# Taking sums of squares of later weights along with the projections, and giving VectorE two attention units a head

## The chip, the cores and the metric

The kernel runs on one core of one Trainium2 chip, in one launch. The metric is the device time of one execution in microseconds (us). Comparisons are made between runs on the same chip.

## The reference

Two layers, each an attention block and a gated block, over x of 2048 rows by 448 columns, all in float32. The weights are the same in both layers.

```python
def A(x, wqkv, wo):            # 16 heads of 28
    q, k, v = split(x @ wqkv)
    p = softmax(q @ k.T * 28 ** -0.5)
    return (p @ v) @ wo
def B(x, w_gate, w_up, w_down): # 448 -> 1792 -> 448
    return (sigmoid(x @ w_gate) * (x @ w_up)) @ w_down
for layer in range(2):
    x = x + A(layernorm(x), wqkv, wo)
    x = x + B(layernorm(x), w_gate, w_up, w_down)
```

## The kernel before

The 2048 rows are 4 blocks of 512, each 4 tiles of 128. Every product is made from float16 parts: an operand is scaled by a power of two and cut into a high and a low part, and three products of parts are added up in PSUM. The order of the instructions on each engine is the order in which the program calls them; there is no scheduler. An engine runs its queue in order and waits by semaphores.

A layer runs through four stages: `project` (queries, keys and values), `attend`, `out_project` and `gated`.

**project.** `qk(b, blk, fill, before)` makes the queries and keys of block b as 7 products of 128 columns (11 matmuls each). After each product ScalarE writes the high part and its squares, VectorE the low part (L723) and the larger of two halves of the squares (L727), SyncE stores both parts in DRAM (`qk_scr`), and then the entry of `fill` for that product is called, which is other work put in at that place. Products go in turn through 4 PSUM banks, so a product waits until the one four before it has been read. Three products later TensorE adds up the squares (`norm_products`, L701 and L704); the last three of a block are added up in `finish`, which is called as `fin` inside a later step. `vals(b, blk, after)` makes the values of the block's four tiles, and calls entries of `after` in the same manner. In layer 0 blocks 0 and 1 are turned by TensorE; blocks 2 and 3 are normed, transposed in 32x32 pieces on VectorE (`squares`), stored in DRAM (`store`, L317), gathered back as columns (`gather`, L325 and L327) and cut into parts by ScalarE and VectorE (`ready`, L210 to L216). The order is qk(0), vals(0), qk(1), vals(1), qk(2), qk(3), vals(2), vals(3). The guard for the exponent is computed from the norms during vals(2), and attention starts behind vals(3).

**attend.** For 16 heads and 16 key tiles of 128 there are 4 units, one for each block of queries: 1024 units of 128x512. TensorE makes the scores of three units at a time (`score`, L1129), and ScalarE takes their exponential in one instruction (L1144). FEW tells for layer 0 how many units of each head go to VectorE instead, 1, 2 or 3 (3 in layer 1 throughout); ASIDE gives for each number the key tile at which the unit is begun, and the key tile and query block that it is: `score_aside`, ten VectorE instructions (L1154 to L1163). `mix` multiplies the probabilities of a key tile with its values (L1180), some two groups behind the scores. An aside unit uses the PSUM bank in which the sums of the previous head stood and those of the next will stand. `finish(h)` turns and divides the head's sums on VectorE (L1209 to L1215). When `mix` is through with key tile c, counted through all heads to 256, it calls `along(c)`.

**Prepare.** In layer 0 `along(c)` also runs the preparation of the later weights. `Prepare.__init__` writes a list of steps with the key tile at which each is due. First come 12 steps that measure: wo, four pieces of w_down and seven pieces of w_gate beside w_up, each read on GpSimd's DMA queue, with a sum of squares on VectorE (L1018, two for a gate-and-up piece) and a copy of it (L1020). They lie 4 or 5 key tiles apart. Then `sizes` adds up over the partitions on GpSimd (L1032) and VectorE makes the powers of two. Then 22 steps that split: wo, 7 pairs of w_down rows, and 14 of w_gate and w_up columns, 5, 8 and 7 key tiles apart. Each is read on GpSimd's queue, summed, scaled and cut on VectorE (L1012, L1070, L221, L226) and stored (`gu_parts`, `dn_parts`, `o_parts`).

`big` hands out 19 buffers of 8 KB a partition, the one longest free first; a DMA into a buffer waits on its queue until the readers before it are done.

## Time and profile before

| what | us |
|---|---|
| median of three runs | 1918.15 |
| range of the three | 1917.75 to 1919.35 |
| the profiled execution | 1918.24 |
| its span, first to last instruction | 1916.4 |
| TensorE busy | 1897.9 |
| VectorE busy | 1412.8 |
| ScalarE busy | 1366.0 |
| GpSimd busy | 240.6 |

A row of the timeline gives the start, the time, the engine, the line, the operation, out<-in, the count, and in brackets the idle time ahead of it and what ended it. A row of groups gives the line, engine, operation, tiles, shape and count, then the busy time and the mean ns of one, then the idle time ahead. A row of windows gives for a stretch the busy time and count for each engine, then the granted clock of TensorE, the busy share of the DMA engines and GB/s. In rows of one line's durations these are ns, least, median and most. Engines: PE TensorE, PEld its weight loads, DVE VectorE, ACT ScalarE, POOL GpSimd, SP SyncE. TensorE's granted clock was 0.997.

### The profile page before, as it was taken

How to read it: one execution, taken by the hardware profiler on the slowest of the kernel's cores; microseconds unless marked ns; L12 is line 12 of the kernel's file. 1: busy time of each engine (PE TensorE's matmuls, PEld its weight loads, DVE VectorE, ACT ScalarE, POOL GpSimd, SP SyncE). 2: the span in 40 equal slices, each digit the busy share in tenths (PEclk: the TensorE clock that was granted, in tenths of full speed). 3: DMA queues.
4: the chain of work that ended last, by engine and by line, in shares of the span. 5: the costliest groups of instructions: out<-in, count | busy, mean ns of one | idle time of the engine just before them, and what ended most of it. 6: DMA issues, size and time to landing. Idle time of an engine off the chain costs nothing. (4 is left out here: it accounts for less than half of the span.)

```text
span 1916.4 us, 56353 instructions
## 1 busy us (share of the span) xinstructions
PE 1897.9 (99%) x24317; PEld 1405.8 (73%) x24317; DVE 1412.8 (74%) x2816; ACT 1366.0 (71%) x1742; POOL 240.6 (13%) x467
## 2 busy tenths in 40 slices
PE   9999999999999999999999999999999999999999
PEld 4455655555566798999954568778888777899998
DVE  7648798687877598788663487778778667887764
ACT  5569999999983455454344799999999645555541
POOL 2013312232001111212100000000000011211110
PEclk9999999999999999999999999999999999999999
DMA  5575555345313657656634312122111235665752
GB/s 173 165 207 162 155 157 149 117 144 149 92 62 92 235 189 263 219 221 236 232 94 132 89 51 51 28 51 51 41 37 66 75 98 215 216 270 198 270 204 90
DMA packets 107298, 275.20 MB, mean 144 GB/s; under 512 B 12766, under 2 KB 63086, under 8 KB 106912
## 3 DMA queue, kind: packets, MB, share of 16 engines
q0 software_dynamic: 33088, 165.74, 24.5%
q1 hardware_dynamic: 73616, 105.54, 19.3%
q8 instruction: 192, 3.15, 0.7%
q14 instruction: 66, 0.54, 0.1%
q10 hardware_dynamic: 336, 0.23, 0.0%
HBM read 213.39 MB, written 50.73 MB: 138 GB/s over the span
## 5 line engine op out<-in xcount | busy, mean ns | idle before, releaser
L1144 ACT ACTIVATE prob_s<-sc 128x1536 f32<-128x1536 f32 x659 | 892.7, 1484 | 6.7 <-PE sc L1129 3.3
L1180 PE MATMUL acc<-prob_s,val_s 128*32 128x256 f32 (+3 forms) x7754 | 590.1, 383 | 0.0
L1129 PE MATMUL sc<-qp_s 114*32 114x512 f16 x7896 | 575.8, 379 | 0.0
L545 PEld LDWEIGHTS <-gu_s 128*128 128x128 f16 x4368 | 428.0, 98 | 60.3 <-issue 8.1
L1129 PEld LDWEIGHTS <-qp_s 114*32 114x32 f16 x8192 | 309.9, 96 | 176.3 <-issue 78.2
L1180 PEld LDWEIGHTS acc<-prob_s,val_s 128*32 128x32 f32 x7754 | 317.9, 110 | 100.8 <-issue 7.6
L545 PE MATMUL chain<-xwide_s,gu_s 128*128 128x256 f16 x2016 | 249.0, 273 | 4.1 <-DMA gu_s<-gu_parts 4.0
L1454 PE MATMUL dnp<-dn_s,hparts_s 128*128 128x224 f16 x2100 | 235.5, 259 | 0.0
L1454 PEld LDWEIGHTS <-hparts_s 128*128 128x128 f16 x2100 | 202.1, 98 | 4.8
L1527 ACT COPY one_q<-chain 128x256 f32<-128x256 f32 x224 | 82.0, 372 | 132.0 <-PE chain L545 131.3
L1160 DVE SCALAR_TENSOR_TENSOR power_q<-power_q,expo_q 128x512 f32<-128x512 f32 x222 | 153.7, 692 | 7.6
L545 PE MATMUL side<-xshort_s,gu_s 128*128 128x256 f16 x1120 | 142.1, 274 | 3.0 <-DVE one_q L1543 2.7
L530 PE MATMUL qkp<-xhl_s,wqk_s 128*128 128x512 f16 x616 | 138.0, 379 | 0.7 <-DVE xhl_s L509 0.3
L1543 DVE TENSOR_TENSOR one_q<-side,one_q 128x512 f32<-128x512 f32 x112 | 72.0, 684 | 83.4 <-PE side L545 83.4
L530 PEld LDWEIGHTS <-wqk_s 128*128 128x128 f16 x616 | 60.0, 98 | 70.1 <-ACT wqk_s L223 1.0
L1209 DVE STREAM_TRANSPOSE oturned_q<-acc 128x512 f32<-128x512 f32 x32 | 22.9, 717 | 118.4 <-PE acc L1180 118.4
L1345 POOL DMA_DIRECT2D gu_s<-gu_parts x104 | 56.0, 540 | 365.7 <-PE side L545 183.3
L545 PE MATMUL side<-xwide_s,gu_s 128*128 128x256 f16 x672 | 92.3, 274 | 0.0
L1407 ACT CAST hparts_s<-hsums_q 128x256 f16<-128x256 f32 (+1 forms) x144 | 68.4, 489 | 33.1 <-DVE hsums_q L1419 20.6
L722 ACT ACTIVATE qkhl_q<-qkp 128x512 f16<-128x512 f32 x56 | 33.2, 593 | 75.0 <-PE qkp L530 71.6
L1180 PE MATMUL acc<-power_q,val_s 128*32 128x256 f32 (+3 forms) x278 | 86.4, 393 | 0.0
L1554 ACT ACTIVATE one_q<-one_q 128x512 f32<-128x512 f32 x56 | 35.3, 630 | 71.3 <-DVE one_q L1543 71.2
(209 smaller groups left out, 2291.0 us busy)
## 6 DMA issues: line engine op xcount, KB each, us to landing
gu_s<-gu_parts POOLq DMA_DIRECT2D x104, 800.0 KB, 6.0
dn_s<-dn_parts POOLq DMA_DIRECT2D x50, 784.0 KB, 7.2
qp_s<-qk_scr SPq DMA_DIRECT2D x96, 224.0 KB
qk_scr<-qkhl_q SPq DMA_DIRECT2D x56, 256.0 KB
gu_parts<-pack_s POOLq DMA_DIRECT2D x14, 800.0 KB, 4.2
xt_scr<-xs_s SPq DMA_DIRECT2D x48, 224.0 KB
xraw_s<-xt_scr SPq DMA_DIRECT2D x12, 768.0 KB
qp_s<-qk_scr SPq DMA_DIRECT2D x64, 112.0 KB
```

The costliest lines, as they stand in the source:

```text
L530: nc.tensor.matmul(pm, w, x, start=(i == 0), stop=(i == len(terms) - 1))
L545: nc.tensor.matmul(pm, a, x, start=(first and i == 0), stop=(i == len(terms) - 1), skip_group_check=True)
L1129: nc.tensor.matmul(ps[32 * j:32 * j + 32, :], hd.k[:, keys], hd.q[:, qb * W:(qb + 1) * W], start=True, stop=True, tile_position=(0, 32 * j))
L1144: nc.scalar.activation(prob[:, 0:n, :], ps[:, 0:n, :], AF.Exp, scale=exp_scale)
L1160: nc.vector.scalar_tensor_tensor(p, p, c[k], y, op0=ALU.add, op1=ALU.mult)
L1180: nc.tensor.matmul(acc[qb * VC:(qb + 1) * VC, s], v[:, kc % TB, h, :], probs[c * NB + qb][:, s], start=(kc == 0 and a == 0), stop=(kc == N ...
L1345: queue.dma_start(self.gu[-1][m], gu_parts[p, m])
L1407: nc.scalar.copy(to[:, :, 0], a)
L1454: nc.tensor.matmul(pm, a[:, x, t], w[:, p, y], start=(begin and n == 0 and (j == 0 or alone)), stop=(n == 2), skip_group_check=True)
L1527: nc.scalar.copy(to, pm)
L1543: nc.vector.tensor_tensor(one[m], side[m], one[m], op=ALU.add)
L1554: nc.scalar.activation(out, v, AF.Sigmoid, scale=gate_scale)
```

## The change

The 12 measuring steps leave attention and go into the projections of layer 0, as a class `Measure`. Its reads are put at the value products of block 0 (six: wo, the four of w_down, the first gate-and-up piece) and at qk(2) (the other six). Its sums are put at the value products of block 1 (wo and the first of w_down), at qk(2) (five) and at qk(3) (five). Of a gate-and-up piece, the gate's squares are summed on VectorE and the up's on ScalarE, and one reduction on VectorE adds up the latter. `ready` of block 3 moves from the second and third product of qk(2) to the third and fourth. `fin` of block 1 stays where it was.

In attention, `sizes` is due at key tile 6 and the first split at 7; splits of w_down are 11 key tiles apart and those of gate and up 10, so that the last is due at 219 and the end at 229. FEW becomes two units for every head but the last, which keeps three: 33 in all, where it was 26.

```diff
@@ -63,7 +63,7 @@
 
 
 ASIDE = {1: ((6, 15, 1),), 2: ((4, 10, 3), (9, 15, 1)), 3: ((4, 9, 3), (8, 13, 1), (12, 15, 2))}
-FEW = "2221212111111233"
+FEW = "2222222222222223"
 
 
 TAIL = (0, 1, 3, 2, 5, 4, 6)
@@ -731,7 +731,8 @@
                 qrt.put(hl)
                 late.append(lambda i=i, sq=sq: norm_products(i, sq))
                 if i < len(fill) and fill[i]:
-                    fill[i]()
+                    for do in fill[i] if isinstance(fill[i], tuple) else (fill[i],):
+                        do()
 
             def finish():
                 while late:
@@ -799,10 +800,12 @@
                 b1.turned_low()
 
             fill = [idle, idle, lambda: b1.norm([0, 1]), lambda: b1.norm([2, 3]), idle, scaled]
-            along_values = {0: lambda: (b1.parts(), turned([0, 1])),
-                            1: lambda: (turned([2, 3]), big.put(b1.xn)),
-                            2: lambda: (fin(), b2.norm()),
-                            3: lambda: (b2.squares(), b2.store())}
+            tell = Measure()
+            add = tell.add
+            along_values = {0: lambda: (b1.parts(), turned([0, 1]), tell.read(2)),
+                            1: lambda: (turned([2, 3]), big.put(b1.xn), tell.read(2)),
+                            2: lambda: (fin(), b2.norm(), tell.read()),
+                            3: lambda: (b2.squares(), b2.store(), tell.read())}
         else:
             ones_of_values()
             fill = [idle, lambda: b1.ready(0, 1), lambda: b1.ready(2, 3), b2.norm,
@@ -817,9 +820,17 @@
         else:
             fill = [idle, lambda: b2.ready(0, 1), lambda: b2.ready(2, 3), b3.store]
         fin = qk(1, b1, fill, None)
-        vals(1, b1, {0: b3.gather, 2 if layer == 0 else 1: fin})
-        fin = qk(2, b2, [idle, lambda: b3.ready(0, 1), lambda: b3.ready(2, 3)], None)
-        fin = qk(3, blks[3], [], fin)
+        if layer == 0:
+            more = lambda: add(1)
+            vals(1, b1, {0: b3.gather, 1: add, 2: fin, 3: add})
+            fin = qk(2, b2, [more, more, lambda: (b3.ready(0, 1), tell.read()),
+                             lambda: b3.ready(2, 3), more, more, more], None)
+            fin = qk(3, blks[3], [add] * 5, fin)
+            assert not tell.rows
+        else:
+            vals(1, b1, {0: b3.gather, 1: fin})
+            fin = qk(2, b2, [idle, lambda: b3.ready(0, 1), lambda: b3.ready(2, 3)], None)
+            fin = qk(3, blks[3], [], fin)
         if layer > 0:
             big.put(*wq.qk)
         else:
@@ -883,6 +894,55 @@
                 big.put(wq.v)
 
         return values, heads, last_values
+
+    class Measure:
+
+
+
+        def __init__(self):
+            nc.vector.memset(sums[:, 3:7], 0.0)
+            self.part = cpool.tile([P, 2], F32, name="part", tag="part", bufs=1)
+            self.ups = cpool.tile([P, 7], F32, name="ups", tag="ups", bufs=1)
+            self.junk = big.get("junk", [P, 2048], BF16)
+            self.to_read = deque([("o", 0)] + [("d", j) for j in range(4)] + [
+                ("gu", j) for j in range(7)])
+            self.rows = deque()
+
+        def read(self, n=1):
+            for _ in range(n):
+                kind, j = self.to_read.popleft()
+                t = big.get("raw", [P, 2048])
+                n = {"o": 4, "d": min(4, NF - 4 * j), "gu": 0}[kind]
+                v = t[:, 0:n * D].rearrange("p (s n) -> p s n", n=D)
+                if kind == "gu":
+                    v = t.rearrange("p (w s c) -> p w s c", w=2, s=4)
+                    for i, w in enumerate((w_gate, w_up)):
+                        load_rows(v[:, i], w, j * 2 * P, 2 * P, nc.gpsimd)
+                elif kind == "o":
+                    load_rows(v, wo, 0, D, nc.gpsimd)
+                else:
+                    nc.gpsimd.dma_start(v, w_down[j * 512:j * 512 + n * P, :].rearrange(
+                        "(s p) n -> p s n", p=P))
+                self.rows.append((kind, j, t, n * D))
+
+        def add(self, read=0):
+            kind, j, t, n = self.rows.popleft()
+            m, n = {"o": (3, n), "d": (6, n), "gu": (4, 1024)}[kind]
+            v = t[:, 0:n]
+            nc.vector.tensor_tensor_reduce(self.junk[:, 0:n], v, v, 1.0, sums[:, m:m + 1],
+                                           op0=ALU.mult, op1=ALU.add,
+                                           accum_out=self.part[:, 0:1])
+            nc.vector.tensor_copy(sums[:, m:m + 1], self.part[:, 0:1])
+            if kind == "gu":
+                junk = qrt.get("junk", [P, 1024], BF16)
+                nc.scalar.activation(junk, t[:, 1024:2048], AF.Square,
+                                     accum_out=self.ups[:, j:j + 1])
+                qrt.put(junk)
+            big.put(t)
+            self.read(read)
+            if not self.rows and not self.to_read:
+                nc.vector.tensor_reduce(sums[:, 5:6], self.ups, axis=AX.X, op=ALU.add)
+                big.put(self.junk)
 
     def true_maxima(h):
 
@@ -913,25 +973,16 @@
 
 
         def __init__(self):
-            nc.vector.memset(sums[:, 3:7], 0.0)
-            self.part = cpool.tile([P, 2], F32, name="part", tag="part", bufs=1)
             self.raws, self.packs = big.ring(2), big.ring(2)
             self.halves, self.half = None, 0
-            tiles = [("o", 0)] + [("d", j) for j in range(4)] + [("gu", j) for j in range(7)]
-            order = [(self.measure, what) for what in tiles] + [
-                (self.split, what) for what in tiles[:1] + [("w", p) for p in range(NP)] + [
-                    (w, p) for p in range(NP) for w in ("g", "u")]]
-            self.read(*tiles[0])
-            self.steps = deque()
-            at = 6
-            for i, (do, what) in enumerate(order):
-                then = order[i + 1][1] if i + 1 < len(order) else None
-                self.steps.append((at, lambda do=do, what=what, then=then:
-                                   self.step(do, what, then)))
-                at += ((5 if what[0] == "gu" else 4) if do == self.measure else
-                       {"o": 5, "w": 8}.get(what[0], 7))
-                if i == len(tiles) - 1:
-                    self.steps.append((at, self.sizes))
+            order = [("o", 0)] + [("w", p) for p in range(NP)] + [
+                (w, p) for p in range(NP) for w in ("g", "u")]
+            self.read(*order[0])
+            self.steps = deque([(6, self.sizes)])
+            at = 7
+            for what, then in zip(order, order[1:] + [None]):
+                self.steps.append((at, lambda what=what, then=then: self.step(what, then)))
+                at += {"o": 5, "w": 11}.get(what[0], 10)
             self.steps.append((at, self.end))
             self.pack = None
 
@@ -954,14 +1005,11 @@
                 self.next = big.at(self.raws, "raw", [P, 2048])
             if kind == "o":
                 load_rows(self.view(self.next, kind), wo, 0, D, nc.gpsimd)
-            elif kind == "gu":
-                for i, w in enumerate((w_gate, w_up)):
-                    load_rows(self.view(self.next, kind)[:, i], w, j * 2 * P, 2 * P, nc.gpsimd)
             elif kind == "w":
                 for z in range(2):
                     r = slice((z * NP + j) * P, (z * NP + j + 1) * P)
                     nc.gpsimd.dma_start(self.view(self.next, kind)[:, z], w_down[r])
-            elif kind in "gu":
+            else:
                 v, w = self.view(self.next, kind), {"g": w_gate, "u": w_up}[kind]
                 for z in range(2):
                     c = slice((z * NP + j) * P, (z * NP + j + 1) * P)
@@ -969,30 +1017,20 @@
                                         w[0:384, c].rearrange("(s p) n -> p s n", p=P))
                     nc.gpsimd.dma_start(v[0:64, 3, z], w[384:448, c])
                 nc.gpsimd.memset(v[64:P, 3], 0.0)
-            else:
-                n = self.count(j)
-                nc.gpsimd.dma_start(self.view(self.next, kind)[:, 0:n, :],
-                                    w_down[j * 512:j * 512 + n * P, :].rearrange(
-                                        "(s p) n -> p s n", p=P))
-
-        def count(self, j):
-            return min(4, NF - 4 * j)
 
         def view(self, t, kind):
-            if kind == "gu":
-                return t.rearrange("p (w s c) -> p w s c", w=2, s=4)
             if kind in "gu":
                 return t[:, 0:1024].rearrange("p (s z n) -> p s z n", s=4, z=2)
             if kind == "w":
                 return t[:, 0:2 * D].rearrange("p (z n) -> p z n", z=2)
             return t[:, 0:4 * D].rearrange("p (s n) -> p s n", s=4)
 
-        def step(self, do, what, then):
+        def step(self, what, then):
             raw = self.next
             self.write()
             if then:
                 self.read(*then)
-            do(raw, *what)
+            self.split(raw, *what)
             if what == ("w", 0):
                 big.free.append(self.raws.popleft())
 
@@ -1011,22 +1049,6 @@
                                  (s34[:, 1], l12, s12[:, 1], ALU.subtract)):
                 nc.vector.tensor_tensor(to, a, b, op=op)
             return s12, s34
-
-        def add(self, m, v):
-            junk = big.at(self.packs, "junk", [P, 2048], BF16)
-            n = v.free_size()
-            nc.vector.tensor_tensor_reduce(junk[:, 0:n], v, v, 1.0, sums[:, m:m + 1],
-                                           op0=ALU.mult, op1=ALU.add, accum_out=self.part[:, 0:1])
-            nc.vector.tensor_copy(sums[:, m:m + 1], self.part[:, 0:1])
-
-        def measure(self, raw, kind, j):
-            if kind == "o":
-                self.add(3, raw[:, 0:4 * D])
-            elif kind == "gu":
-                self.add(4, raw[:, 0:1024])
-                self.add(5, raw[:, 1024:2048])
-            else:
-                self.add(6, raw[:, 0:self.count(j) * D])
 
         def sizes(self):
             nc.gpsimd.partition_all_reduce(size[:, 3:7], sums[:, 3:7], channels=P,
```

## The prediction, made before the changed kernel ran

> **What bounds the kernel now.** I read the share of busy time first, then the windows of the two attention stages, then the timeline at their edges, and last the waits and DMA shares of the first projection stage, since the change takes work from one of these stages and gives it to another. Base: the profiled execution took 1918.24 us, its span is 1916.4, and the median of the three runs is 1918.15, so the sum against the execution holds for the median within 0.1.
>
> ```profile
> core 0: us, PE busy (x) PEld busy (x) DVE busy (x) ACT busy (x) POOL busy (x), PEclk, DMA share, GB/s
> 119.10:570.70 451.60, 451.56 (x8140) 259.63 (x8139) 363.46 (x703) 448.63 (x333) 95.73 (x156) 1.00 0.48 141
> 1068.50:1515.10 446.60, 446.60 (x8108) 357.37 (x8107) 344.54 (x572) 444.04 (x326) 0.00 (x0) 1.00 0.18 46
> L1144 ACT ACTIVATE prob_s<-sc 128x1536 f32<-128x1536 f32 x333 | 448.6, 1514 | 3.7 <-DMA qp_s<-qk_scr 3.1 <-PE sc L1129 0.3
> ```
>
> The first two rows are the attention stages of layer 0 and layer 1, from first score product to first output projection. In layer 0 ScalarE runs 333 exponentials back to back, 448.63/333 = 1.347 us each, and sat idle only 3.7 us, of which 3.1 before the first. So ScalarE bounds that stage. Layer 1 does the same products with 48 units beside it on VectorE instead of 26, so with 326 exponentials, and takes 446.6: nearly the floor that TensorE's products set. VectorE is at 363.46/451.6 = 80% in layer 0.
>
> ```profile
> 105.17 0.49 PE L704 MATMUL knorm<-sq_q,ind 128*128 128x256 bf16 x3
> 119.10 1.48 PE L1129 MATMUL sc<-qp_s 114*32 114x512 f16 x24
> 67.40:104.40 37.00, 37.00 (x181) 17.51 (x179) 16.08 (x35) 19.46 (x33) 0.00 (x0) 1.00 0.47 140
> ```
>
> The projection ahead of it is TensorE's: in its second half (last row) TensorE is busy 37.0 of 37.0 us, VectorE only 16.08. The squared-norm products of the last block start at 105.17, in the middle of the value products, and the first scores follow the value products directly at 119.10. Whatever makes TensorE wait before 119.10 is added to the whole.
>
> **The change: fewer exponentials.** FEW goes from a sum of 26 to a sum of 33, so 7 more units of 128x512 leave ScalarE. 1024 - 26 = 998 units are 332.7 groups of three, 1024 - 33 = 991 are 330.3. The gain is 2.33 x 1.347 = 3.1 us, and the stage would take 448.5. That is above the 446.6 of layer 1, so TensorE doesn't yet cap it. The 0.6 us of other idle time of ScalarE is the most that could come on top: 3.7.
>
> **What VectorE has to do for it.**
>
> ```profile
> 214.89 0.75 DVE L1154 TENSOR_SCALAR expo_q<-aside,base 128x512 f32<-128x512 f32 x1 [2.86 <-PE aside L1129]
> 221.18 1.28 DVE L1018 CUSTOM_DVE_ANT_0 junk_s<-raw_s,sums 128x1024 bf16<-128x1024 f32 x1
> 222.72 1.29 DVE L1018 CUSTOM_DVE_ANT_0 junk_s<-raw_s,sums 128x1024 bf16<-128x1024 f32 x1
> 142.75 2.08 DVE L1018 CUSTOM_DVE_ANT_0 junk_s<-raw_s,sums 128x1792 bf16<-128x1792 f32 x1
> 145.05 2.08 DVE L1018 CUSTOM_DVE_ANT_0 junk_s<-raw_s,sums 128x1792 bf16<-128x1792 f32 x1
> L1018 DVE CUSTOM_DVE_ANT_0 junk_s<-raw_s,sums x19: 1145/1285/2085, 142.7 to 225.8; 128x1024 bf16<-128x1024 f32 x14, 128x1792 bf16<-128x1792 f32 x4, 128x896 bf16<-128x896 f32 x1
> 376.70 0.72 DVE L1209 STREAM_TRANSPOSE oturned_q<-acc 128x512 f32<-128x512 f32 x1 [6.86 <-PE acc L1180]
> 380.29 0.42 DVE L1012 TENSOR_TENSOR sums_q<-raws_s 128x256 f32<-128x256 f32 x1
> 386.06 0.75 DVE L1154 TENSOR_SCALAR expo_q<-aside,base 128x512 f32<-128x512 f32 x1
> 233.45 0.17 DVE L238 TENSOR_SCALAR pw<-size 128x4 int32<-128x4 int32 x1 [6.15 <-POOL size L1032]
> ```
>
> From start to start, a unit takes 6.29 us (214.89 to 221.18), a sum with its copy 1.54 (1024 wide), 2.30 (1792 wide) or 1.4 (896 wide, 1.145 and the same 0.25), the end of a head 3.6 and one gate or up split 5.8. Seven units add 44.0 us; 14 x 1.54 + 4 x 2.30 + 1.4 = 32.2 leave, so VectorE rises by 12 to 375 of 448.5, 84%. The sums are now done long before the powers of two are asked for at key tile 6, so the 6.15 us in which VectorE waited for GpSimd's all-reduce should go too; that was no one's critical wait.
>
> Spreading is what makes room: a gate or up split falls every 10 key tiles, not every 7. A key tile lasts 448.5/256 = 1.75 us, a head 28.0; a head with two splits holds 2 x 6.3 + 3.6 + 2 x 5.8 = 27.8, and averages over neighbours are 25.6. A unit is asked for six key tiles before its use and the products trail the scores by 2.25 groups, 10.5 + 3.0 = 13.5 us; a unit behind a split that has just begun is ready after 5.8 + 6.3 = 12.1. Thin, but it holds; I cost it at nothing. If this cover fails, TensorE waits. The last split ends at key tile 229 instead of 220, and the output weights are first read in the last head, from tile 242: nothing.
>
> **What the projection gets.** Twelve reads go onto GpSimd's queue from the first values on. GpSimd idles 14.30 and 9.05 us ahead of its two norm steps there (first rows below), a read of six issues lasts 3.63 (rows further below), and each read takes a buffer already free, or freed as named below, so the norm steps behind them aren't held up. ScalarE gets seven squares of 1024.
>
> ```profile
> 44.17 0.20 POOL L283 TENSOR_SCALAR rs<-mv 128x4 f32<-128x4 f32 x1 [14.30 <-DVE mv L280]
> 54.53 0.19 POOL L283 TENSOR_SCALAR rs<-mv 128x4 f32<-128x4 f32 x1 [9.05 <-DVE mv L280]
> L599 ACT ACTIVATE junk_s<-wraw_s 128x1792 bf16<-128x1792 f32 x2 | 3.4, 1682 | 0.0
> 66.71 0.41 DVE L740 TENSOR_REDUCE peaks<-qnorm 16x1 f32<-16x256 f32 x1
> 77.79 1.14 ACT L210 CAST xhl_s<-xraw_s 128x512 f16<-128x512 f32 x2 [3.15 <-DMA xraw_s<-xt_scr]
> 78.44 1.29 DVE L211 TENSOR_TENSOR xhl_s<-xraw_s,xhl_s 128x512 f16<-128x512 f32 x2 [3.47 <-ACT xhl_s L210]
> 82.06 0.69 DVE L723 SCALAR_TENSOR_TENSOR qkhl_q<-qkp,qkhl_q 128x512 f16<-128x512 f32 x1
> 82.87 0.69 DVE L723 SCALAR_TENSOR_TENSOR qkhl_q<-qkp,qkhl_q 128x512 f16<-128x512 f32 x1
> ```
>
> A square of 1024 lies under the 1.68 us of 1792, about 1.0, and ScalarE has 37.0 - 19.5 = 17.5 us free in the second half: nothing. VectorE gets 2.30 x 4 + 1.4 + 7 x 1.54 = 21.4 us into 37.0 - 16.1 = 20.9 of idle time. So it becomes full, and order decides. Ahead of block 3's parts stand, from 66.7: four sums (9.2), the peaks (0.8) and three evacuation pairs of 0.81 (82.06 to 82.87), 12.4 in all, to 79.1. The gathered block 3 used to land at 77.79 and now is asked for one product later. From its landing: one cast (0.6), four low parts (2.6), 11 evacuation pairs (8.9), a 896 and seven 1024 sums (12.2), peaks (0.8), 25.1 us. The last squares must be there when the norm products start, at 105.2. So the gather may land as late as 80.1 at no cost, and from there each microsecond is one that TensorE waits.
>
> ```profile
> 66.00:69.00 3.00, 3.00 (x18) 1.66 (x17) 1.42 (x3) 1.42 (x4) 0.00 (x0) 1.00 0.93 213
> 69.00:72.00 3.00, 3.00 (x16) 1.36 (x14) 0.36 (x1) 1.14 (x3) 0.00 (x0) 1.00 0.82 186
> 75.00:78.00 3.00, 3.00 (x16) 1.35 (x15) 0.00 (x0) 0.21 (x1) 0.00 (x0) 1.00 1.03 331
> 65.56 3.43 SPq L317 DMA_DIRECT2D xt_scr<-xs_s  x4
> 72.30 0.38 SPq L325 DMA_DIRECT2D xraw_s<-xt_scr  x1
> 173.05 0.78 POOL L203 DMA_DIRECT2D raw_s<-in_B_w_gate_dram  x1 [3.88 <-DVE sums L1020]
> 176.68 0.78 POOL L203 DMA_DIRECT2D raw_s<-in_B_w_gate_dram  x1
> raw_s<-in_B_w_down_dram POOLq DMA_DIRECT2D x1, 896.0 KB, 13.5
> ```
>
> Block 3's store (from 65.56) fills the DMA engines to 0.93 and 0.82, its gather (issued 72.30 when the store has landed) to 1.03. The second gate-and-up read takes block 2's gathered buffer, free at 66.7, so its six issues (3.63 us, 173.05 to 176.68) go out beside that store; the third takes the buffer that the store reads, and goes out beside the gather. Each is 2 x 384 KB, 0.79 MB: 2.4 us of all engines at 331 GB/s, 4.2 at 186. Before, nothing on GpSimd's queue ran there. Bounds: 0 if the reads fit the gaps, 8.4 us if both go wholly ahead at the slow rate. That sharing delays is shown by the last row: 896 KB took 13.5 us to land in the crowded stretch at 119. I take shares alike: 2.4 on the store, and half of it, 1.3, on the gather, whose rival is issued only bit by bit: it lands at 81.5 and costs 1.4 us.
>
> The Trainium skill (DMA: Bandwidth & Descriptors, Queues, rings and completion order) says that each DMA engine goes round between the queues it has work for, a packet at a time. By that rule this read is not behind the gather but between its packets, which speaks against the change; no row here shows the two queues at once in this stretch.
>
> Sum: 1918.2 - 3.1 + 1.4 = 1916.5.
>
> **The rivals.** (1) No collision: the reads fit the gaps, the gather lands by 80.1, and ScalarE's 0.6 us of idle time may go too: 1914.5 to 1915.1. For it: 20 us windows before show DMA shares of a half on average (0.47 in the row above). Against: the shares at that very place. (2) Slower: the reads go ahead. The place is block 3's store and gather, the price 1 us for each microsecond past 80.1, and it decides from 80.1 + 3.1 = 83.2; at 8.4 us late it lands at 86.2, costs 6.1 and gives 1921.2. More reads follow at once, so it could be still later. For it: the 13.5 us landing. Against: the gather's own queue is served meanwhile. The round-robin rule of the Trainium skill, named above, with larger packets in the reads than in the store, leans to this one. (3) VectorE's queue in attention: heads with two splits have 0.2 us to spare, so operations 10% longer would put each some 2.5 us behind; at two to three such heads 5 to 8 us, less the gain: 1921 to 1925. Against: layer 1's 344.54 busy us with three units a head stall nothing. (4) That the change doesn't do what it says: TensorE, not ScalarE, paces layer 0. Then 451.6 would stay: 1919.6. The 333 exponentials with 0.6 us between them speak against it.
>
> **How the numbers follow.** About 0.2% (3.8 us, so 1914.4 and 1922.1) is what a measurement of this kernel can tell from no change. Chances: forecast 0.46 (own range 1915.1 to 1918.2), (1) 0.20, (2) 0.23, (3) 0.08, (4) 0.03. Faster by over 0.2% is the lower half of (1), with the spread of the runs: 0.12. Slower is half of (2), most of (3) and what I can't see, 0.22. The range, 1914.4 to 1923, leaves out a tenth at each end.
>
> **What would show it.** Right: 331 exponentials in a stage of some 448.5 us; no wait of TensorE on an `aside` unit; the L210 wait for xraw in the third product longer than before, landing near 81.5; TensorE waiting about 1.4 us on sq at the last norm products; first scores at about 120.5. Wrong: first scores at 119.1 (then 1) or past 122 (then 2); a stage still over 450 us (then 3 or 4), told apart by ScalarE's idle time.

## The result, and the profile after

The changed kernel takes 1922.63 us (median of 8 runs, 1920.91 to 1926.01), the kernel before 1915.94 beside it (median of 8, the three of the forecast among them). The ratio of the runs is 1.0038, 95% interval 1.0026 to 1.0049: slower by some 7 us. The forecast was 1916.5; 1922.63 lies inside its range, which reached up to 1923 for the rivals' sake, and the sign was wrong. The profiled execution took 1920.91, its span is 1917.8.

The attention of layer 0 gained more than forecast. From first scores to first output projection it takes 446.86 us where it took 451.61, with 331 exponentials, and TensorE is busy throughout (windows and the group of the exponential, changed kernel):

```profile
core 0: us, PE busy (x) PEld busy (x) DVE busy (x) ACT busy (x) POOL busy (x), PEclk, DMA share, GB/s
125.66:572.52 446.86, 446.86 (x8109) 265.79 (x8108) 374.38 (x715) 444.23 (x331) 64.38 (x107) 1.00 0.40 117
L1166 ACT ACTIVATE prob_s<-sc 128x1536 f32<-128x1536 f32 (+1 forms) x331 | 444.2, 1515 | 3.4 <-PE sc L1151 3.1 <-DMA qp_s<-qk_scr 0.3
```

But the first scores come at 125.66, not 119.10: 6.56 us are lost ahead of attention. The timeline of SyncE's queue and of ScalarE shows block 3's store, gather and first cast:

```profile
66.76 3.46 SPq L317 DMA_DIRECT2D xt_scr<-xs_s  x4
77.97 0.38 SPq L325 DMA_DIRECT2D xraw_s<-xt_scr  x1
83.17 1.14 ACT L210 CAST xhl_s<-xraw_s 128x512 f16<-128x512 f32 x2 [4.59 <-DMA xraw_s<-xt_scr]
```

The gather is issued at 77.97 (72.30 before) and the cast starts at 83.17 (77.79). From the store's issue to the gather's it takes 11.2 us instead of 6.7: the reads did delay the store, by 4.5 us where 2.4 were forecast. What follows from it for TensorE is small, one wait for VectorE at the norm products of block 2 (timeline of TensorE):

```profile
92.65 0.27 PE L704 MATMUL knorm<-sq_q,ind 128*128 128x256 bf16 x1 [0.35 <-DVE sq_q L727]
```

The long wait comes 17 us behind that one (timeline of ScalarE, then of TensorE, then windows; `...` marks rows left out):

```profile
101.95 1.06 ACT L938 ACTIVATE junk_q<-raw_s 128x1024 bf16<-128x1024 f32 x1 [0.63 <-DMA raw_s<-in_B_w_up_dram]
...
106.84 1.06 ACT L938 ACTIVATE junk_q<-raw_s 128x1024 bf16<-128x1024 f32 x1 [2.59 <-DMA raw_s<-in_B_w_up_dram]
...
107.90 0.58 ACT L722 ACTIVATE qkhl_q<-qkp 128x512 f16<-128x512 f32 x1
108.51 0.63 ACT L725 ACTIVATE sq_q<-qkhl_q 128x512 bf16<-128x512 f16 x1
109.04 0.58 ACT L722 ACTIVATE qkhl_q<-qkp 128x512 f16<-128x512 f32 x1
109.66 0.63 ACT L725 ACTIVATE sq_q<-qkhl_q 128x512 bf16<-128x512 f16 x1
```

```profile
109.51 0.27 PE L704 MATMUL knorm<-sq_q,ind 128*128 128x256 bf16 x1 [1.99 <-DVE sq_q L727]
110.66 0.37 PE L704 MATMUL knorm<-sq_q,ind 128*128 128x256 bf16 x1 [0.88 <-DVE sq_q L727]
```

```profile
102.00:105.00 3.00, 3.00 (x16) 1.42 (x15) 2.64 (x7) 2.22 (x4) 0.16 (x1) 1.00 0.97 331
105.00:108.00 3.00, 2.52 (x15) 1.32 (x14) 1.15 (x3) 1.16 (x3) 0.00 (x0) 1.00 0.39 132
108.00:111.00 3.00, 0.61 (x3) 0.35 (x3) 2.42 (x8) 2.22 (x4) 0.00 (x0) 0.82 0.19 66
111.00:114.00 3.00, 3.00 (x12) 1.22 (x10) 0.81 (x4) 0.54 (x1) 2.03 (x2) 0.61 0.80 228
109.90:113.31 3.41, 2.65 (x8) 1.13 (x8) 1.88 (x8) 0.93 (x2) 1.34 (x2) 0.50 0.72 207
```

ScalarE waits 2.59 us, until 106.84, for the last up piece, and behind that square stand the last two evacuations of queries and keys. Their squares are what TensorE's last norm products wait for: TensorE is busy 0.61 of 3 us. Then its granted clock is 0.82 and 0.61 in the means of two 3-us windows; the last row, cut to the fall itself, has 0.50 for 3.41 us. That is 1.7 us of lost work if TensorE has work throughout; here it had 2.65 us of it, so 1.3 to 1.7. The 6.56 us add up as follows: 1.2 are there already at block 3's store (66.76 against 65.56), 0.9 come between the store and the first of the last norm products (107.25 against 105.17), and 4.5 behind that, which are the 2.9 us of gap and the clock.

The loss ahead of attention and the gain in it make 6.56 - 4.75 = 1.8 us, and the spans differ by 1.4, but the medians by 6.7. The two executions don't stand for their medians: that of before took 2.3 us more than its median of 1915.94, that of after is the shortest of its 8. And one stage that wasn't touched has grown: from the first output projection to layer 1's first scores (570.71 to 1068.47 before, 572.52 to 1072.81 after) 500.29 us instead of 497.76.

### The profile page after: what moved, and what is told of

Same layout as the page of the kernel before. It is cut to its first block, busy times and chain, and to the rows that moved or that the text cites. A ratio compares the mean times of both kernels' runs of the same rounds, so it can differ in the third digit from the quotient of the medians.

```text
span 1917.8 us, 56351 instructions
## 1 busy us (share of the span) xinstructions
PE 1893.8 (99%) x24285; PEld 1348.4 (70%) x24285; DVE 1442.2 (75%) x2866; ACT 1368.1 (71%) x1754; POOL 239.0 (12%) x467
## 5 line engine op out<-in xcount | busy, mean ns | idle before, releaser
L1166 ACT ACTIVATE prob_s<-sc 128x1536 f32<-128x1536 f32 (+1 forms) x657 | 887.7, 1485 | 7.3 <-PE sc L1151 3.4
L1202 PE MATMUL acc<-prob_s,val_s 128*32 128x256 f32 (+3 forms) x7700 | 574.2, 384 | 0.0
L1151 PE MATMUL sc<-qp_s 114*32 114x512 f16 x7868 | 557.0, 379 | 0.0
L1151 PEld LDWEIGHTS <-qp_s 114*32 114x32 f16 x8192 | 281.5, 96 | 195.2 <-issue 81.9
L1202 PEld LDWEIGHTS acc<-prob_s,val_s 128*32 128x32 f32 x7700 | 282.8, 110 | 133.4 <-issue 11.1
L1182 DVE SCALAR_TENSOR_TENSOR power_q<-power_q,expo_q 128x512 f32<-128x512 f32 x243 | 168.2, 692 | 8.3
L1202 PE MATMUL acc<-power_q,val_s 128*32 128x256 f32 (+3 forms) x300 | 94.2, 396 | 0.0
L1176 DVE TENSOR_SCALAR expo_q<-aside,base 128x512 f32<-128x512 f32 x81 | 60.6, 749 | 28.2 <-PE aside L1151 27.7
```

The costliest lines, as they stand in the source:

```text
L1151: nc.tensor.matmul(ps[32 * j:32 * j + 32, :], hd.k[:, keys], hd.q[:, qb * W:(qb + 1) * W], start=True, stop=True, tile_position=(0, 32 * j))
L1166: nc.scalar.activation(prob[:, 0:n, :], ps[:, 0:n, :], AF.Exp, scale=exp_scale)
L1176: nc.vector.tensor_scalar(y, ps, base2[:, 0:1], -126.0, op0=ALU.mult, op1=ALU.max)
L1182: nc.vector.scalar_tensor_tensor(p, p, c[k], y, op0=ALU.add, op1=ALU.mult)
L1202: nc.tensor.matmul(acc[qb * VC:(qb + 1) * VC, s], v[:, kc % TB, h, :], probs[c * NB + qb][:, s], start=(kc == 0 and a == 0), stop=(kc == N ...
```

## The experiments

Ratios are to the kernel before on the same chip, with 95% intervals, from 5 to 12 runs of each kernel and 15 to 33 of the kernel before. Stage times are those of one traced execution of each kernel.

### Both kernels once more

> The changed kernel once more, unchanged, for a second trace and times on the same chip as the other experiments. If the loss is where the first trace has it: first scores 124.5 to 126.5 us, ScalarE waiting for the last up piece, attention of layer 0 at 447, time 6 to 7 us above the kernel before. Rival: the first trace's gap was that one execution's, and first scores come at 120 to 122.

> The kernel before once more, unchanged, for a second trace on this chip. Theory C1 (the kernel without the third products' reads is no faster than before, 1.0002, although its first trace ends 5.6 us earlier, since TensorE's gap in layer 0's gated products near 730 us is longer with two units a head, 3.2 to 3.6 us against 2.0, and each long gap is followed by a lowered clock): here the gap near 730 is 2.0 again, and attention 451 to 452. Rival C2: the gap there varies from run to run whatever the kernel, and comes out at 3 us or more here in this trace or in the next.

Changed again: 1.0032 (1.002 to 1.0044), first scores at 125.81, ScalarE's wait for the up piece 3.0 us, TensorE's gap 3.5, attention 446.85. Before again: 0.9995 (0.9986 to 1.0004), first scores at 119.53, attention 452.83. The loss at 107 to 111 us is the kernel's, not that execution's.

### The units and the sums apart

```diff
-FEW = "2222222222222223"   # in the changed kernel
+FEW = "2221212111111233"
```

> The changed kernel with only the old count of units beside ScalarE in layer 0's attention (26, not 33); sums and splits stay as changed. Theory A (the loss lies in the projection ahead of the first scores, attention gained 4.7 us): attention of layer 0 back at 451 to 452 us, first scores still near 125.7, time 4 to 5 us above the changed kernel, near 1927. Rival B (VectorE with two units a head makes attention pay somewhere later): attention stays near 447 or the time falls below the changed kernel's 1922.6.

1.0035 (1.0024 to 1.0047). Attention takes 450.62 us: against the two traces of the kernel before (451.61 and 452.83) the sums' leaving is worth 1.0 to 2.2 us, and against the changed kernel the units 3.76. Yet the time is not 4 to 5 us above the changed kernel but level with it, within some 3 us. The first scores, expected near 125.7, come at 123.04 in this trace; nothing ahead of them differs from the changed kernel, whose three other traces here and below have 125.66, 125.81 and 124.53, so executions vary by that much. Most of attention's gain doesn't reach the end; the reason is found further below, in the wait near 730 us, which is 2.08 here and 3.4 in the changed kernel.

```diff
-FEW = "2221212111111233"   # in the kernel before
+FEW = "2222222222222223"
```

> The kernel before with only the new count of units beside ScalarE (33, not 26), sums and splits staying in attention at their old places. If the sums had to leave for the units: VectorE is over-full in the first heads (a sum of 2 x 1.54 us each 8.8 us, or 2.3 each 7, plus two units of 6.3 in 28), TensorE waits on units, attention of layer 0 at 452 to 460 and the time 1 to 9 us above before. Rival: VectorE's queue absorbs it, attention at 447 to 449 and first scores at 119, time 1910 to 1913, and the move of the sums was not needed. By C1 the gap near 730 us is 3.2 to 3.6 us here.

1.0074 (1.006 to 1.0088). Attention's window and TensorE's waits in it:

```profile
119.26:580.15 460.89, 452.11 (x8109) 264.79 (x8108) 406.00 (x773) 445.19 (x331) 95.10 (x156) 0.99 0.47 138
PE aside L1129 <- DVE oturned_q L1209: 8.8, 2, 4.6
409.66 0.60 PE L1129 MATMUL aside<-qp_s 114*32 114x512 f16 x4 [4.16 <-DVE oturned_q L1209]
499.38 0.62 PE L1129 MATMUL aside<-qp_s 114*32 114x512 f16 x4 [4.62 <-DVE oturned_q L1209]
```

VectorE is busy 406 of 461 us, and twice TensorE can't begin an aside unit, because VectorE comes late to empty the bank with the previous head's sums: 8.8 us, and some 5 more in the lowered clock behind these waits. So the units alone don't pay; the time is above the forecast of 1 to 9 us. But the two waits are not in the first heads, where the expectation had them. They stand at 410 and 499 us, among splits 7 key tiles apart, 180 us and more behind the last sum (228.8 in this trace). What this run shows is that the splits had to be spread; the sums' leaving is what gives them the room. Two units with spread splits and the sums in place were not run.

### What costs in the projection

```diff
# without the reads: each later gate-and-up sum is taken on the first piece again
...
+            if kind == "gu" and self.to_read:
+                self.rows.append(("gu", self.to_read.popleft()[1], t, 0))
# without the sums: every later gate-and-up piece is read, and put back without a sum
...
+            if kind == "gu" and j:
+                big.put(t); self.read(read); return
```

> The six gate-and-up pieces after the first are not read; their sums are taken on the first piece over and over, so VectorE and ScalarE do the same work at the same places (sizes of the later weights then come out wrong). Theory A1 (the pieces land late, ScalarE waits for the last one in order and the last evacuations stand behind it): no wait of ScalarE on its squares, TensorE's gap at 107 to 111 us goes, first scores at 119 to 121, time 4.5 to 6.5 us below the changed kernel, 1916 to 1918. Rival A2 (VectorE is full with the sums and evacuates late by itself): gap stays, first scores near 125, time near 1922. Rival A3 (collision with block 3's store and gather): gather lands near 78 again, and the time falls too; told apart from A1 by the next kernel.

> All pieces are read, but no sums are taken of the gate-and-up pieces after the first, neither on VectorE nor on ScalarE (sizes then come out wrong). Theory A1 (ScalarE's in-order wait for the last piece): nobody waits for the late pieces, first scores at 119.5 to 121.5, time 1916 to 1918.5. Rival A2 (VectorE full): the same 1916 to 1918.5, so that with the kernel without the reads the two are told apart. Rival A3 (the reads delay block 3's gather and this costs): gather lands near 83 as in the changed kernel and the time stays near 1921 to 1922.6.

Without the reads 1.0002 (0.9992 to 1.0013), first scores at 119.99; without the sums 1.0016 (1.0007 to 1.0025), 120.24. The window of 72 to 102 us in the first and the cast of block 3 in the second:

```profile
72.00:102.00 30.00, 30.00 (x146) 14.10 (x145) 28.85 (x62) 24.38 (x43) 0.00 (x0) 1.00 0.41 135
```

```profile
81.86 1.14 ACT L210 CAST xhl_s<-xraw_s 128x512 f16<-128x512 f32 x2 [3.70 <-DMA xraw_s<-xt_scr]
```

With all sums and no late data VectorE is full, 28.85 of 30 us, and TensorE still doesn't wait: rival A2 falls. With all reads and no sums the gather lands 4.1 us later than in the kernel before, and TensorE doesn't wait behind it: the late gather alone is not the price, so A3 falls. Only both together cost. That fits A1, late data with an engine that waits for them in order; it would also fit a late gather together with a full VectorE, which neither kernel has. Against the latter speak the changed kernel's windows, in which VectorE is busy only 1.15 of 3 us just ahead of the gap, and the next three kernels.

```diff
-            fin = qk(3, blks[3], [add] * 5, fin)
+            fin = qk(3, blks[3], [add] * 2, fin)
...
+            vals(2, blks[2], {0: guard_of_norms, 1: add, 2: add, 3: (worst_of_heads, add)})
```

> Nothing is left out: the last three sums move from the last query-and-key products into the third block's value products, behind the last evacuations of queries and keys. Theory A1: the last maxima no longer stand behind the late piece, TensorE's gap ahead of the last norm products goes, and with it the lowered clock; first scores 120 to 121.5, time 4 to 5.5 us below the changed kernel, 1917 to 1918.5, and attention unchanged at 447. Rival A3 (collision with block 3's store and gather, or clock at the start): no more than 1 us below the changed kernel.

That is the late placement. The mended kernel places the three sums as its expectation says:

> Nothing is left out: the changed kernel with its last three sums behind the last evacuations (one between the bound's power and the guard, one beside the third block's second value tile, one beside the last block's first value tile), and GpSimd's clearing of the guard's zeros ahead of the norms. Theory A1: first scores at 119.8 to 120.8 us, half a us to 1.5 earlier than with the first late placement (121.33), attention 447, time 1 us below that kernel, 1916 to 1917. Without C1's cost it would be 1911 to 1913.

The late placement gives 1.0013 (1.0004 to 1.0022), first scores at 121.33; the mended kernel 1.0015 (1.0005 to 1.0025), 120.88. Both have attention's 447 to 448 and no gap ahead of the last norm products, although block 3's gather is late in the mended kernel too (its cast starts at 82.34, against 83.17 in the changed one, and TensorE waits 0.49 us behind it). So the last three sums' place is worth 3 to 4 us. The second placement, expected 1 us below the first, isn't faster. In its place another wait has grown (late placement):

```profile
119.15 0.36 PE L555 MATMUL vp<-wv_s,xhl_s 128*128 128x448 f16 x1 [1.55 <-DVEq L877]
```

TensorE waits at the branch ahead of attention for VectorE, which has sums before it. It is 1.14 us in the mended kernel; the kernel before and the changed one wait 0.63 there, for ScalarE.

```diff
+                for _ in range(7):                      # in the kernel before, layer 0, qk(3)
+                    nc.scalar.activation(junk, x[:, 0:2, :], AF.Square)
-        fin = qk(3, blks[3], [], fin)
+        fin = qk(3, blks[3], [idle, idle, idle, idle, hold], fin)
```

> The kernel before, with seven needless squares (128x896, some 0.9 us each) on ScalarE between its fifth and sixth evacuation of the last block's queries and keys in layer 0. No read, no sum and no work of VectorE is added: only ScalarE stands in front of the last two evacuations, as it stood in the changed kernel while it waited for the last piece. Theory A1: the sixth evacuation starts near 106.5 instead of 102, TensorE waits 2.5 to 3.5 us ahead of the last norm products, the granted clock falls after it in some executions (1.7 us more); first scores at 122 to 124.5, time 3 to 5 us above before. Rival: TensorE has other value products to go on with, first scores stay below 120.5 and the time within 1 us.

1.0017 (1.0008 to 1.0026), first scores at 123.14. No read and no sum is added, ScalarE alone is held (windows):

```profile
102.00:105.00 3.00, 3.00 (x18) 1.57 (x16) 0.00 (x0) 3.00 (x5) 0.00 (x0) 1.00 0.00 0
105.00:108.00 3.00, 0.80 (x5) 0.38 (x4) 2.17 (x7) 2.31 (x5) 0.00 (x0) 1.00 0.17 58
108.00:111.00 3.00, 3.00 (x12) 1.27 (x10) 0.90 (x4) 0.54 (x1) 1.95 (x2) 0.63 0.83 237
111.00:114.00 3.00, 3.00 (x14) 1.42 (x13) 0.74 (x1) 0.64 (x2) 0.34 (x1) 0.81 0.92 213
```

The gap is there again, 2.2 us, and the clock's fall after it, 0.37 x 3 + 0.19 x 3 = 1.7 us, all of it in work. Together 3.9; its first scores are 3.6 to 4.0 us late (119.10 and 119.53 before). A ScalarE that stands still in front of its last two evacuations is enough for the loss.

### Where attention's gain went

The mended kernel should have been 2 to 3 us faster than before and was 2 to 3 slower. In the gated products of layer 0 TensorE waits once for a gate-and-up read, near 730 us, in every kernel. Its wait in the traces (us): 1.98, 1.82, 1.89 and 2.08 with 26 units, 3.16 to 3.57 in six kernels with 33. Two rows of the timeline for each kernel, the read's issue on GpSimd and the product that had waited for it; first the kernel before, then the changed one:

```profile
723.70 0.53 POOL L1345 DMA_DIRECT2D gu_s<-gu_parts  x1 [9.20 <-DMA xt_scr<-xs_s]
730.78 0.83 PE L545 MATMUL chain<-xwide_s,gu_s 128*128 128x256 f16 x6 [1.98 <-DMA gu_s<-gu_parts]
```

```profile
725.07 0.53 POOL L1367 DMA_DIRECT2D gu_s<-gu_parts  x1 [9.32 <-DMA xt_scr<-xs_s]
733.46 0.83 PE L545 MATMUL chain<-xwide_s,gu_s 128*128 128x256 f16 x6 [3.40 <-DMA gu_s<-gu_parts]
```

The same read is used 8.39 us after its issue instead of 7.08. Three kernels varied what might matter:

```diff
-FEW = "2222222222222223"   # in the mended kernel, one at a time
+FEW = "2222222222222222"
+FEW = "2222222122222122"
+            big.free.rotate(3)   # at the end of layer 0's attention
```

> The mended kernel with 32 units beside ScalarE (two in every head) in place of 33. Attention 447 to 449, first scores near 120.9. By C1 (the gap near 730 us goes with the count of units) it stays 3.2 to 3.6 us, time near 1917.5; if it depends on the placing alone it may fall to 2.0, and then 1913 to 1916.

> The mended kernel with 30 units beside ScalarE. Attention 447.5 to 449 (one exponential more, 1.35 us), first scores near 120.9; the gap near 730 us 3.2 to 3.6 by C1, 2.0 if it goes with something else; time 1917 to 1919, or 1914 to 1916 with the short gap.

> The mended kernel with the list of free large buffers turned by three at the end of layer 0's attention, so that the products after it use other buffers for their weights; no work changes. If the wait near 730 us hangs on which buffers the reads land in, it changes from 3.4 us (towards 2.0 or elsewhere); if not, it stays at 3.2 to 3.6 and the time near 1917.5.

32 units: 1.0017 (1.0008 to 1.0026), wait 3.21. 30 units: 1.0027 (1.0015 to 1.0038), wait 2.93. Other buffers: 1.0024 (1.0014 to 1.0033), wait 3.64. The buffers are not it. The DMA queues in the window from the read's issue to its use tell more, first of the kernel before, then of the changed one:

```profile
q0 software_dynamic: 220, 1.30, 48.5%
q1 hardware_dynamic: 480, 0.92, 41.7%
```

```profile
q0 software_dynamic: 302, 1.72, 53.3%
q1 hardware_dynamic: 480, 0.92, 38.1%
q8 instruction: 1, 0.02, 0.8%
```

In the changed kernel one packet of the instruction queue falls into the read, and its time is 0.8% of 16 engines' 8.39 us: 1.07 us of one engine. If the read is spread over the engines and ends with the last of them, such a packet is long enough for most of the 1.31 us; the trace doesn't tell the engines apart, so this step is inferred. In all 14 traces at hand this packet lies 0.5 to 1.5 us ahead of the read's issue with 26 units, and 4.5 to 6.5 us after it with 30 to 33. What the number of units changes is TensorE's program: `mix` cuts the products of a key tile where the pace of the exponentials tells it to, and up to the end of attention the program has 16 matmuls fewer with 33 units, 12 fewer with 30 or 32. (These products take float32 operands as they are, not float16 parts, and the trace has two rows for each: 4000 against 4032 up to the first output projection.) So these were put back, or taken out of the kernel before:

```diff
+                if layer == 0 and n > 1 and halved < 4:          # changed and mended; 8 for the last
+                    n, halved = 1, halved + 1                    # 4 more pieces of 4 matmuls
...
+                if layer == 0 and i % 4 == 0 and n < 4 and halved < 4 ...:  # before
+                    halved += 1; break                                     # 4 pieces fewer
```

> The mended kernel with four value products of layer 0's attention cut in two more pieces (one column block and the rest), so that TensorE's stream up to the end of attention is 16 instructions longer and as long as that of the kernel before; no other work changes. Theory D1 (a packet of the instruction queue takes an engine of the gate-and-up read near 730 us): the packet falls ahead of the read again, the read lands after 6.9 to 7.1 us, TensorE waits about 2.0 us instead of 3.4; with the lowered clock that follows less often, the time falls by 1.4 to 4 us against the mended kernel, to 1913.5 to 1916. Rival D2 (the wait goes with the units beside ScalarE in another way): the wait stays at 3.2 to 3.6 and the time at 1917.5.

> The changed kernel with the same 16 instructions more. D1: wait near 730 us 2.0, first scores still near 125.7, time 1.4 to 4 us below the changed kernel, 1917 to 1919.5. D2: wait 3.4, time 1920.6 to 1922.6.

> The kernel before with four of its cut value products left whole, so that the stream up to the end of attention is 16 instructions shorter, as long as that of the changed kernel; 26 units, sums and splits as before. D1: the packet falls into the read, which lands after 8.1 to 8.5 us; TensorE waits 3.2 to 3.6 us near 730; the time rises by 1.4 to 4 us above before. D2: the wait stays 2.0 and the time that of before.

> The mended kernel with 32 instructions more. D1: the packet comes still earlier, ahead of the read; wait near 730 us 2.0, time as with 16 more, unless the packet meets another read that TensorE waits for (then that wait grows by 1 to 1.5 us). D2: wait 3.4, 1917.5.

| kernel | the program's matmuls to the end of attention, against before | wait near 730, us | ratio |
|---|---|---|---|
| mended | -16 | 3.40 | 1.0015 (1.0005 to 1.0025) |
| mended, longer | 0 | 1.96 | 0.9994 (0.9985 to 1.0003) |
| mended, longer by 32 | +16 | 1.89 | 0.9999 (0.9988 to 1.0009) |
| changed (second runs) | -16 | 3.37 | 1.0032 (1.002 to 1.0044) |
| changed, longer | 0 | 1.99 | 1.0019 (1.001 to 1.0028) |
| before | 0 | 1.82 | 0.9995 (0.9986 to 1.0004) |
| before, shorter | -16 | 3.40 | 1.002 (1.0009 to 1.0031) |

The kernel before, with nothing changed but four products left whole, is 0.2% slower; its first scores (118.71) and its attention (452.24) are those of before. Its queues in the read's window and its product:

```profile
q0 software_dynamic: 305, 1.74, 53.4%
q1 hardware_dynamic: 480, 0.92, 38.9%
q8 instruction: 1, 0.02, 0.8%
```

```profile
730.15 0.83 PE L546 MATMUL chain<-xwide_s,gu_s 128*128 128x256 f16 x6 [3.40 <-DMA gu_s<-gu_parts]
```

D1 holds: in the five later traces (that of the last kernel below among them) the packet lies ahead of the read's issue in the four with a wait of 1.9 to 2.0 us (by 1.3 to 2.4 us), and 6.2 us after it in this one. The pairs of the mended kernel and of the kernel before are clear of the noise; in that of the changed kernel the intervals overlap.

The Trainium skill (Advanced Engine Details and Errata, ISA Cache) states that instructions are cached in lines of 16 KB, which hold 256 instructions. The profile's table of queues agrees, 3.15 MB in 192 packets of 16.4 KB over the whole of the kernel before:

```profile
q8 instruction: 192, 3.15, 0.7%
```

The time moves by more than the 1.4 us of the wait: by 1.3, 2.1 and 2.5 thousandths in the three pairs of the table, 2.5 to 4.8 us. The clock takes part: it falls right at the wait or behind it in 8 of the 11 traces with a wait of 2.9 us or more, and in 2 of the 8 with a shorter one, by 1.7 us of work or, in three of them, twice that. An estimate over all runs, from the granted clock that is recorded with each, gives the time lost to a lowered clock as 4.4 us in the mended kernel and 3.7 in the longer one, 6.4 and 6.1 in the changed pair, 2.8 to 3.9 in the kernel before and 5.4 in the shorter one. So the clock goes the same way in each pair, but whether wait and clock are all of the difference isn't settled: two sets of runs of the same kernel differ by 1.1 us in this figure.

In the last kernel the mended one, with its 16 matmuls put back, takes its last sum behind the branch:

```diff
-            vals(3, blks[3], {0: add}, range(2))
+            vals(3, blks[3], {}, range(2))                        # ahead of the branch
...
+        vals(3, blks[3], {2: add} if layer == 0 else {}, [2], 1 if layer == 0 else 7)
```

> The mended kernel with 16 instructions more, with its last sum moved behind the branch that precedes attention, beside the last block's third value tile; nothing is left out. If the 1.1 us that TensorE waits for VectorE's branch is the sum's: that wait falls to 0.6, first scores near 120.4 us, attention 447 to 448.5, time 0.5 us below the kernel with the sum ahead, 1912.5 to 1914. Rival: the sum then delays the first exponentials or the last block's values, and attention takes 1 us more: no gain.

0.9995 (0.9986 to 1.0004), 1913.68 us against 1914.98. First scores at 120.22, the wait at the branch is 0.63 us as in the kernel before, attention 447.99. The rival has a part of it: attention gives back 0.3 us. In the time nothing shows: the kernel with the sum ahead of the branch had 0.9994, and the 0.5 us of the forecast are less than these runs tell apart. These two are the best versions. They are some 7 us faster than the changed kernel (0.9994 and 0.9995 against 1.0032 and 1.0038); against the kernel before the intervals still hold 1.

## Why the prediction was wrong, point by point

- *Fewer exponentials, 3.1 us.* Right and undersized: 4.75. Two whole exponentials go, 2.7 us, and the last of the 331 has one unit where the last of the 333 had two, 0.4 us: that is the 3.1 of the sum. The rest, 1.6 us, is that the whole ones follow each other a little faster (1.345 us each instead of 1.349) and that 0.3 us of idle time went. The kernel with the old count of units has 1.0 to 2.2 us of gain from the sums' leaving alone; by what way the sums slowed the exponentials isn't shown.
- *Two units a head and spread splits cost nothing.* Right: TensorE waits on no unit, and VectorE is busy 374.4 of 446.9 us (forecast 375 of 448.5). That the splits must be spread for it is shown by the kernel with the units alone. (The rival on VectorE's queue was added up wrongly: 5 to 8 us less the gain of 3.1 is 1920.1 to 1923.1, not 1921 to 1925.)
- *VectorE becomes full, and each microsecond of the gather past 80.1 is one that TensorE waits.* This step failed as the mechanism. VectorE was full (28.85 of 30 us without the late reads) and kept pace. The gather was in at 83.2, 3.1 us past the point, and TensorE waited 0.35 us behind it instead of 3.1; in the mended kernel with 32 matmuls more, where it came at 83.4, 1.22. The sign that the forecast had named, a wait on the squares at the last norm products, did come, with 2.9 us instead of 1.4; but ScalarE held it up, not VectorE's full queue. That the place fits is luck.
- *A square of 1024 on ScalarE, about 1.0 us, into 17.5 us of idle time: nothing.* This is the step that failed. The size was right (1.04 and 0.19 for its reading out), the cover was not. The sum asked if ScalarE had time, not when its data come and what stands behind it in its queue: the last two evacuations. The last piece came 2.6 us late for it. Its price of 4.5 us, 2.9 of gap and the rest of clock, stands against 1.4 forecast for the whole projection. In the same place the trace showed that late reads are slow (13.5 us to land at 119), and it was used for the gather only.
- *Each read takes a buffer already free.* GpSimd waited 6.51 us at 78.47 for the store of block 3, whose buffer the third of these reads takes, as forecast; but then the last DMA of each half of a piece waited for an earlier read, 5.4 us in all, which was not (groups of GpSimd's issues between 66 and 112 us):

```profile
L203 POOL DMA_DIRECT2D raw_s<-in_B_w_gate_dram x6 | 4.7, 784 | 18.3 <-PE knorm L704 11.7 <-DMA xt_scr<-xs_s 6.5
...
L206 POOL DMA_DIRECT2D raw_s<-in_B_w_up_dram x6 | 3.1, 523 | 2.5 <-DMA raw_s<-in_B_w_up_dram 2.5
L206 POOL DMA_DIRECT2D raw_s<-in_B_w_gate_dram x6 | 3.1, 523 | 2.9 <-DMA raw_s<-in_B_w_gate_dram 2.9
```

  So the later pieces were issued late, and landed late.
- *The rival of the reads going ahead* named 1921.2 with the gather at 86.2. The first half was right, the reads did push the store (by 4.5 us) and with it the gather (issued 5.7 us later), the second was not: the price was paid by the last piece. The round-robin of the Trainium skill (DMA: Bandwidth & Descriptors, Queues, rings and completion order) agrees with a store that is delayed and not blocked; for the time of the kernel it didn't decide.
- *Missing altogether:* a code packet that meets a read 600 us later. The forecast held every stage after attention as unchanged, at nothing and without a reason. By the kernel with 16 matmuls put back it cost the changed kernel 1.3 thousandths, 2.5 us, with overlapping intervals; the two clear pairs have 4.0 and 4.8.

Of the changed kernel's 6 to 7 us, the place of the last sums is 3 to 4 and the code packet 2.5 to 5: together about as much as the loss. That leaves attention's gain to account for. With both cured the last version's first scores are 0.7 to 1.1 us later than before and its attention 3.6 to 4.8 us shorter, 2.5 to 4.1 us to gain. It measures 1.0, and its interval reaches 2.7; where the rest is, if it is missing, isn't settled.

## What to carry to other kernels

An operation put into an idle engine is free only if its data are there when its turn comes, since everything behind it waits too; put work on late data behind the last thing that others wait for. Add up a change's price over the whole kernel: here one stage won 4.7 us and the whole lost 6.7, in part because a stream 16 matmuls shorter let a code packet meet a read that was already waited for. When a gain vanishes, compare the waits of the untouched stages between several traces.

## What the runs showed of the hardware

- A gap of TensorE can be paid twice. After gaps of 2.0 to 4.6 us the granted clock fell in many executions, to 0.50 for 3.41 us, which is 1.7 us of lost work where TensorE has work throughout (0.63 and 0.81 in the held kernel's windows). Near 730 us gaps of 2.08 (old count of units) and 1.99 (changed, longer) were followed by it, one of 1.98 (the kernel before) and one of 3.40 (before, shorter) not. The Trainium skill (TensorE: Matmul & The Clock Gate, What's actually happening) gives half rate when cold and a window of 3413 ns, by which a fall costs 1.7 us, as an estimate: the traces agree. It ties the fall to an idle window of that length; here a gap of 2.0 us was enough at times.
- Code is loaded while the program runs: 192 packets of 16.4 KB on the queue shown above, each some 1.1 us of one DMA engine. In the 11 traces in which one of them falls into the read near 730 us, the read is used 7.9 to 8.6 us after its issue, in the 8 others 6.8 to 7.1; putting 16 matmuls in or taking 16 out moved the packet, and the wait with it.
